# Moving a DMA transpose of two steps in four past the output projection, and packing the last output projections into a 64-column pass and a 32-column pass

## Chip, cores, metric

The kernel runs on one core of one Trainium2 chip. The metric is the device time of one execution in microseconds, the median over several runs. The core has five engines that are named here by their short names: PE (matrix multiply; "PEld" is its weight load), DVE (vector), ACT (activation), POOL (general purpose) and SP (sync). SP computes nothing; it issues DMAs in order. POOL's queue also issues DMAs in this kernel. Each engine works through its own list in order and waits on semaphores.

## What is computed

One sequence of 2048 tokens, width 640, goes through two blocks. The first is an attention with a recurrent memory of 8 tokens: the sequence is cut into 64 segments of 32 tokens, and each segment needs the memory that the segment before has produced.

```python
for s in range(n_seg):                       # 64 segments, one after the other
    h = concat([mem, xs])                    # 8 memory tokens + 32 tokens
    q, k, v = h @ Wq, h @ Wk, h @ Wv         # 640 -> 32 heads of 128
    p = softmax(mask(q @ k.T * Dh ** -0.5))
    o = (p @ v) @ Wo                         # 32*128 -> 640
    mem = o[:8]                              # goes into the next segment
    outs.append(o[8:])
h  = x + outs                                # x was layer-normed before attention
h2 = h + (relu(ln(h) @ W_gate) * (ln(h) @ W_up)) @ W_down   # 640 -> 1728 -> 640
```

All tensors are bf16. [...]W_gate, W_up and W_down are loaded over the attention weights at the end.

## The kernel before

**How the program is made.** Every instruction is recorded by `add(engine, function, reads, writes)`. `solve` turns the reads and writes into semaphore waits, and `run` gives each engine its instructions in the order in which they were recorded. So the order in the source is the order on each queue, and there is no scheduler. Most copies have line L461 (ACT) or L463 (DVE), most DMAs L357, and the DMA transposes L360, because helpers record them: tell them apart by their tiles.

**A step.** The loop `for s in range(NSEG)` (L893) does one segment per step; steps 2 to 62 take 13.1 to 14.9 us each. PE's order in a step is: K projection of the memory tokens and of 24 "rider" tokens of later segments (`project(a, ks, 1, ...)`), Q projection, two fifths of the V projection, `pick_mem` (takes the memory's queries out of `tok`), the rest of V, `scores`, a filler in five parts, `pv_mem`, `trans_om`, the output projection `wo_pass` (L641, 128 matmuls of 160 columns, four side by side in 32-column tiles), and `pv_x`. The filler differs by s % 4: for 2, 3 and 0 it is the K, Q and V projection of 32 extra tokens (`extra_units`), for 1 it is `woe_pass`, the output projection of the first 8 tokens of four earlier segments.

**Instruction lines.** PE's program is cut into lines of 256 instructions that are loaded while it runs (queue 8 of the trace, 16,384 bytes each). `align` pads the program so that a line ends at a chosen place in each `wo_pass`: after 98 of its 256 instructions for s % 4 = 1, after 111, 123 and 146 for 2, 3 and 0.

**The riders' queries.** A step projects the queries of its riders into two PSUM banks, `to_tok` copies them to `tok[2]` (ACT) and `tok[3]` (DVE), the DMA transpose `trans_q` turns these into `QS` (32 heads, 32 tokens), and `evac_q` copies the riders' part on ACT into the ring `Qr`, from which `scores` reads it two steps later or more. In SP's queue a step has three transposes in this order: `KS` (keys), `oT` (attention output of the step before, from `ox`), `QS`; then the loads of `loads()`. On ACT, `evac_q` stands after `exp_x` of the same step. `tok[2]` and `tok[3]` are written again by `extra_units` in steps with s % 4 = 2 and 3, and by the next step's Q projection in all steps. `QS` is used once more by the extra tokens' queries: transposed at the end of a step with s % 4 = 3 and copied in the next by the `late_q` list. The `late` list holds what is recorded just after the next step's `trans_ox`.

**The end of the attention.** Step 62 issues `load_gate_up` on POOL's queue: `xn2T`, `Wg`, `Wu`. Step 63 has K and V projections only. After its `pv_x` come: the output projection of segment 62 (`wo_pass` with `QS`, in two halves), the first gate and up product `gate_up(0, 0)`, the output projection of segment 63 (`wo_pass` with `oT`), `gate_up(0, 1)`, the first 8 tokens of segments 60 to 63 (`woe_pass` with `oTe`), `gate_up(0, 2)`, and then the gated block without a break, four blocks of 512 tokens. The stores to `attn_d` go through POOL's queue, and `ln2_load` fetches rows of it for the gated block.

Of the kernel before, what the change touches and what calls it, by code (L numbers as in the profile page):

```python
# [5 lines left out]
BF16 = mybir.dt.bfloat16  # L6
# [35 lines left out]
class _Graph:  # L42
# [164 lines left out]
def build_kernel(nc, A_x, A_mem0, A_Wq, A_Wk, A_Wv, A_Wo, A_seg_len, B_W_gate, B_W_up, B_W_down, out):  # L207
    _, S, D = A_x.shape
# [60 lines left out]
    act_e = [ar.alloc(f"act_e{i}", [128, DC, 32], BF16) for i in range(2)]  # L269
    tokp = [ar.alloc(f"tok{i}", [128, 1024], BF16) for i in range(2)]  # L270
    tok = [tokp[i // 2][:, 512 * (i % 2):512 * (i % 2) + 512] for i in range(4)]
# [25 lines left out]
    def bank(b):  # L297
        return ps[:, b * 512:(b + 1) * 512]
# [17 lines left out]
    def B(n):  # L316
        return ("B", n)
# [317 lines left out]
    def wo_pass(bk, mark=None, src=oT, keys=((("oT", "m"), ("oT", "x")), (("oT", "n"),)), halves=(0, 1)):  # L635
        for hf in halves:
            def f(pe, hf=hf):
                for hb in ORDER[16 * hf:16 * hf + 16]:
                    w = Wo[:, head_of(hb), :].rearrange("p (c g j) -> p g c j", g=4, j=32)
                    for gg in range(4):  # L640
                        i = pe.matmul(bank(bk)[32 * gg:32 * gg + 32, 0:160], src[:, hb, :], w[:, gg],  # L641
                                      start=(hb == ORDER[0]), stop=(hb == ORDER[31]), skip_group_check=True)
                return i
            op = add("pe", f, r=list(keys[hf]) + [("Wo", hf)], w=[B(bk)])
            if hf == 0:
                op.mark = mark

    def woe_pass(bk, part):

        def f(pe):  # L650
            for i in part:
                for q in range(4):
                    hb = 16 * (q // 2) + i
                    w = Wo[:, head_of(hb), :].rearrange("p (c g j) -> p g c j", g=4, j=32)
                    ins = pe.matmul(bank(bk)[32 * q:32 * q + 32, 0:320], oTe[:, hb, :],  # L655
                                    w[:, 2 * (q % 2):2 * (q % 2) + 2], start=(i == 0), stop=(i == 15),
                                    skip_group_check=True)
            return ins
        add("pe", f, r=oTe_keys + [("Wo", 0), ("Wo", 1)], w=[B(bk)])

# [41 lines left out]
    def trans_pe(dst, keys):  # L702

        flat = ox[:].rearrange("p k g d -> p (k g d)")
        for n, (b, eng) in enumerate(((T0, "act"), (T1, "dve"))):
            def f(pe, n=n, b=b):
                for k in range(4):
                    o = 512 * n + 128 * k
                    ins = pe.matmul(bank_bf(b)[:, k * 128:(k + 1) * 128], flat[:, o:o + 128], ident[:, :],
                                    is_transpose=True)  # L710
                return ins
            add("pe", f, r=[("ox", 0), ("ox", 1), ("ident",)], w=[B(b)])
            copy_op(eng, dst[:, 16 * n:16 * n + 16, :], slots(b, 0, 32)[:, 0:16, :], [B(b)], keys)

# [5 lines left out]
    def attn_keys(i):  # L720
        return [("attn", s) for s in range(4 * i, 4 * i + 4)] + [("attne", i, dg) for dg in range(2)]

# [162 lines left out]

    def woe_store(b):
        for dg in range(2):
            dma(bass.AP(attn_d, 128 * b * D + 320 * dg, [[SEG * D, 4], [D, M], [1, 320]]),
                bass.AP(at, 32 * dg * D, [[D, 32], [1, 320]]), r=[("at",)] + [("attn", 4 * b + j) for j in range(4)],
                w=[("attne", b, dg)], eng="pool")  # L890

    late, late_q = [], []
    for s in range(NSEG):  # L893
# [20 lines left out]
        if s > 0:  # L914
# [20 lines left out]
            late_q = []  # L935
            if nr and s < NSEG - 2:
                trans_q()
# [137 lines left out]

    def rows(bk, p, s):
        wo_rows(bk, wtok[p], ("wtok", p), "act")
        store_attn(wtok[p], ("wtok", p), s)

# [11 lines left out]
    mask_x()  # L1091
    trans_pe(QS, [("QS",)])
    pv_x(s, P0)
    copy_op("act", oTe[:, :, M * ((s - 1) % 4):M * ((s - 1) % 4) + M], QS[:, :, 0:M], [("QS",)], [("oTe", (s - 1) % 4)])
    norm_x(P0)
    wo_pass(BQ[1], None, QS, [[("QS",)]] * 2, (0,))
    trans_pe(oT, [("oT", "m"), ("oT", "n"), ("oT", "x")])
    wo_pass(BQ[1], None, QS, [[("QS",)]] * 2, (1,))
    rows(BQ[1], 0, s - 1)
    copy_oTe(s)  # L1100
    gate_up(0, 0)
    for i in range(4, 8):
        ln2_load(i)
    dma(h_rows[0][:, :, :], h_d[:, :].rearrange("(u p) d -> p u d", p=128), r=[("h_d", u) for u in range(4)] +
        [("Wdone", 1), ("Wu", DC - 1)], w=[("h", 0, u) for u in range(4)], eng="pool")
    dma(Wd[:, 0:FC - 1, :], B_W_down[0:FM, :].rearrange("(j p) d -> p j d", p=128),
        r=[("Wdone", 1)], w=[("Wd", 0)], eng="pool")
    dma(Wd[FR:128, FC - 1, :], B_W_down[FM:F, :], r=[("Wdone", 1)], w=[("Wd", 1)], eng="pool")
# [92 lines left out]
```

## Time and profile before

| | |
|---|---|
| runs | 1108.61, 1108.92, 1111.25 us; median 1108.92 |
| profiled execution | 1111.65 us, of it the span on the core 1109.9 us |
| mean granted PE clock | 0.992 |
| PE busy | 1054.9 us, 95% of the span |
| DVE, ACT, POOL busy | 608.7, 365.7, 290.5 us |
| DMA transposes and other DMAs of SP and ACT (queue 1) | 267,824 packets, 41.2% of the 16 DMA engines' time |
| steps with s % 4 = 1, 2, 3, 0 | median 13.98, 13.63, 13.34, 13.37 us from the end of one `pv_x` to the next |
| end of the last `pv_x` | 917.06 us; the gated block runs without a break from 932.94 us |

The page has one profiled execution. A group is a line with its engine, its output and inputs, its shape and count, the union of its busy time and the mean of one. "Idle before" is time in which the engine stood still before instructions of the group, with what ended it; "issue" means that nothing in the profile ended it. In the chain of waits, a row is the start, the length, and what took it. PE overlaps matmuls, so "PE busy" is not PE at its peak. Times "into the step" below count from the end of the `pv_x` before.

### The profile page before, as it was taken

To read this page: it belongs to the slowest core of one execution; us is meant where nothing else is said; L and a number is where in the kernel's file an instruction comes from. 1 tells how busy PE (TensorE), PEld (TensorE's weight loads), DVE (VectorE), ACT (ScalarE), POOL (GpSimd) and SP (SyncE) were. 2 spreads that over 40 slices of the span, in tenths; PEclk is the share of its full clock that TensorE was granted. 3 is DMA by queue.
4 is the path that set the end of the run, shared out by engine and by line. 5 is a ranking of instruction groups with operands and counts; after the bars stand their busy time and mean duration, and the time that the engine had idled before them with its cause. 6 is when DMAs were issued, how large, how long until landed. Compare 5 with 4: busy or idle time off the path is not lost.

```text
span 1109.9 us, 56106 instructions
## 1 busy us (share of the span) xinstructions
PE 1054.9 (95%) x28040; PEld 510.8 (46%) x23478; DVE 608.7 (55%) x1673; ACT 365.7 (33%) x794; POOL 290.5 (26%) x583
## 2 busy tenths in 40 slices
PE   4679999999999999999999999999999998999998
PEld 3344544444545454545454445444444454444443
DVE  3245656565556565666666666565656553553532
ACT  1214333433343433333334333334333332231211
POOL 1013333333333332323232323232324151000000
PEclk9979999999999999999999999999999999999999
DMA  9936464646463636465756665554545557132100
GB/s 362 377 84 111 88 109 89 105 90 107 81 110 80 115 79 110 83 123 100 119 103 116 104 114 107 93 92 97 94 92 96 93 159 240 39 80 75 27 18 25
DMA packets 287788, 121.65 MB, mean 110 GB/s; under 512 B 263968, under 2 KB 277184, under 8 KB 287552
## 3 DMA queue, kind: packets, MB, share of 16 engines
q1 hardware_dynamic: 267824, 93.92, 41.2%
q0 software_dynamic: 19312, 23.89, 9.3%
q8 instruction: 202, 3.31, 1.2%
q14 instruction: 34, 0.28, 0.1%
q10 hardware_dynamic: 416, 0.26, 0.1%
HBM read 36.79 MB, written 7.21 MB: 40 GB/s over the span
## 4 chain that ended last, share of the span: by engine, by line
PE 86%; DMA 8%; SPq 3%; issue 1%; POOL 1%; DVE 1%; ACT 1%; DVEq 0%; ACTq 0%
PE ps L419 24%; PE ps L397 23%; PE ps L641 13%; PE ps L1030 10%; PE ps L655 3%; PE ps L679 3%; PE ps L569 3%; PE ps L1062 3%; DMA Wo<-in_A_Wo_dram 3%; SPq L357 3%; PE ps L606 2%; DMA QS<-tok 2%; DMA KS<-tok 2%; PE ps L450 2%; PE ps L621 1%
## 5 line engine op out<-in xcount | busy, mean ns | idle before, releaser
L419 PE MATMUL ps<-W,act_r 128*32 128x512 bf16 x4277 | 399.1, 384 | 8.8 <-DMA W<-in_A_Wv_dram 2.5
L397 PE MATMUL ps<-W,act_r 128*32 128x512 bf16 x3603 | 356.9, 379 | 0.3
L357 POOL DMA_DIRECT2D Vr<-Vp x376 | 187.6, 506 | 449.7 <-ACT Px L588 396.9
L419 PEld LDWEIGHTS ps<-W,act_r 128*32 128x32 bf16 x4277 | 121.5, 97 | 262.2 <-issue 170.2
L461 ACT ACTIVATE tok<-ps 128x512 bf16<-128x512 f32 x191 | 110.3, 594 | 237.2 <-PE ps L397 204.7
L641 PE MATMUL ps<-Wo,oT 128*32 128x160 bf16 x8192 | 161.8, 236 | 14.6 <-DMA Wo<-in_A_Wo_dram 8.0
L641 PEld LDWEIGHTS ps<-Wo,oT 128*32 128x32 bf16 x8192 | 147.0, 98 | 36.6 <-issue 16.7
L463 DVE CAST tok<-ps 128x512 bf16<-128x512 f32 x131 | 90.5, 691 | 131.5 <-PE ps L397 109.9
L461 ACT ACTIVATE Qr<-QS 128x512 bf16<-128x512 bf16 (+3 forms) x107 | 70.1, 682 | 61.0 <-DMA QS<-tok 60.5
L419 PE MATMUL ps<-W,act_e 128*32 128x512 bf16 x900 | 89.6, 381 | 0.0
L397 PE MATMUL ps<-W,act_e 128*32 128x512 bf16 x900 | 89.1, 379 | 0.0
L552 DVE STREAM_TRANSPOSE TBf<-ps 128x64 f32<-128x64 f32 (+1 forms) x128 | 33.5, 262 | 93.9 <-PE ps L641 93.8
L694 DVE TENSOR_TENSOR ox<-ps,rx 128x512 bf16<-128x512 f32 x128 | 82.4, 685 | 2.2
L461 ACT ACTIVATE Vp<-ps 128x256 bf16<-128x256 f32 (+1 forms) x126 | 48.5, 385 | 104.7 <-PE ps L397 102.2
L357 POOL DMA_DIRECT2D attn_d<-wtok x64 | 46.6, 728 | 126.8 <-ACT wtok L461 126.6
L1045 DVE TENSOR_TENSOR hT<-g,ps 128x512 bf16<-128x512 bf16 (+1 forms) x56 | 38.5, 688 | 53.7 <-PE ps L1030 49.8
L1030 PE MATMUL ps<-xn2T,Wu 128*128 128x512 bf16 x260 | 64.6, 379 | 0.0
L1030 PE MATMUL ps<-xn2T,Wg 128*128 128x512 bf16 x246 | 61.6, 379 | 1.1 <-issue 0.3
L1043 ACT ACTIVATE g<-ps 128x512 bf16<-128x512 f32 (+1 forms) x56 | 32.4, 592 | 89.4 <-PE ps L1030 89.4
L397 PE MATMUL ps<-Wd,hT 128*128 128x320 bf16 x224 | 61.0, 299 | 0.0
L1062 PE MATMUL ps<-Wd,hT 128*128 128x320 bf16 x224 | 61.0, 299 | 0.0
L463 DVE CAST Vp<-ps 128x512 bf16<-128x512 f32 x64 | 44.2, 691 | 30.4 <-PE ps L397 24.5
(114 smaller groups left out, 1145.8 us busy)
## 6 DMA issues: line engine op xcount, KB each, us to landing
Vr<-Vp POOLq DMA_DIRECT2D x124, 48.8 KB, 2.3
W<-in_A_Wk_dram SPq DMA_DIRECT2D x2, 2560.0 KB, 13.2
W<-in_A_Wq_dram SPq DMA_DIRECT2D x2, 2560.0 KB, 29.3
W<-in_A_Wv_dram SPq DMA_DIRECT2D x2, 2560.0 KB, 28.1
Wo<-in_A_Wo_dram SPq DMA_DIRECT2D x2, 2560.0 KB, 28.5
xt<-in_A_x_dram SPq DMA_DIRECT2D x30, 160.0 KB, 3.6
Vr<-Vp POOLq DMA_DIRECT2D x128, 32.5 KB, 1.9
attn_d<-wtok POOLq DMA_DIRECT2D x64, 40.0 KB, 2.9
```

The costliest lines, as they stand in the source:

```text
L357: add(eng, lambda e: e.dma_start(dst, src), r=r, w=w, dma=True)
L397: return pe.add_instruction(mybir.InstMatmult(name=nc.get_next_instruction_name(), engine=mybir.EngineType.PE, ins=[pe.lower_ap(rhs), pe.l ...
L419: ins = pe.matmul(*a, start=(c == 0), stop=(c == DC - 1), skip_group_check=True)
L461: add("act", lambda a: a.activation(dst, src, ACTF.Copy), r=r, w=w)
L463: add("dve", lambda v: v.tensor_copy(dst, src), r=r, w=w)
L552: add("dve", lambda v, lo=lo, hi=hi: v.transpose(TBf[:, lo:hi, :].rearrange("p c t -> p (c t)"), src[:, 32 * lo:32 * hi]), r=[wkey], w=[(" ...
L569: i = pe.matmul(bank((P0, P1)[g % 2])[p:p + (M if a else 32), 40 * k:40 * k + 40], lh, Qr[:, h, q, :], start=True, stop=True, skip_group_c ...
L641: i = pe.matmul(bank(bk)[32 * gg:32 * gg + 32, 0:160], src[:, hb, :], w[:, gg], start=(hb == ORDER[0]), stop=(hb == ORDER[31]), skip_group ...
L694: add("dve", lambda v, kh=kh: v.tensor_tensor(ox[:, :, kh, :], src[:, :, kh, 0:128], ap(rx, kh, [[2, 4], [0, 128]]), ALU.mult), r=[B(b0 + ...
L1030: ins = pe.matmul(bank(bk), w[:, c, lo:lo + 128], xn2T[par][:, c, :], start=(c == 0), stop=(c == DC - 1))
L1045: add("dve", lambda v: v.tensor_tensor(hT[par][lo:128, j, :], g1[gi][lo:128, :], bank(bu)[lo:128, :], ALU.mult), r=[B(bu), ("g1", gi)], w= ...
L1062: i = pe.matmul(*a, start=(j == 0), stop=(j == FC - 1), skip_group_check=True)
```

## The change

Three things are changed in the loop (items 1 to 3), and the end of the attention is rewritten (item 4).

1. In steps with s % 4 = 0 and 1, `trans_q` is recorded after the store of `wo_pass`'s rows instead of after the Q projection, and it waits for the first copy of the new memory into `act_r` (key `"m"`). Its `evac_q` moves into a new list, `late_k`, which the next step records just after its K projection's two `to_tok` copies.
2. The store of `woe_pass`'s rows goes into `late`, so into the next step, and waits for that step's `KS`.
3. In step 62 `load_gate_up` is recorded after `wo_pass` and waits for its first half.
4. After the last `pv_x`, segment 62's 32 tokens and the first 8 tokens of segments 60 and 61 are put side by side into one 64-column tile, `wide`, which lies over the four `tok` buffers. Its product with Wo is 64 matmuls of 320 columns, two side by side. Segment 63 takes `woe_pass` with `oT`. The two `gate_up` products that stood between come after, and `ln2_load`, the load of `h` and of `Wd` wait for the sum `at` of segment 63.

```diff
-    tokp = [ar.alloc(f"tok{i}", [128, 1024], BF16) for i in range(2)]
+    tokb = ar.alloc("tok", [128, 2048], BF16)
+    tokp = [tokb[:, 1024 * i:1024 * i + 1024] for i in range(2)]
...
-    def trans_q():
+    def trans_q(after=()):
         dma_t(QS[:].rearrange("p h t -> p (h t)").rearrange("p (k r) -> p k r", r=128), tokp[1][:, :],
-              [("tok", 2), ("tok", 3)], [("QS",)])
+              [("tok", 2), ("tok", 3)] + list(after), [("QS",)])
...
     def ln2_load(i):
         u = i % 4
-        dma(xt2[u][:, :], x_ap[128 * i:128 * i + 128, :], r=[("Wdone", 1), ("Wu", DC - 1)], w=[("xt2", u)])
+        dma(xt2[u][:, :], x_ap[128 * i:128 * i + 128, :], r=[("Wdone", 1), ("at",)], w=[("xt2", u)])
...
             to_tok(BQ[0], 0, "act")
             to_tok(BQ[1], 1, "dve")
+            for f in late_k:
+                f()
+            late_k = []
...
-            if nr and s < NSEG - 2:
+            qlate = nr and s % 4 < 2
+            if nr and not qlate and s < NSEG - 2:
                 trans_q()
...
-                if s < NSEG - 2:
+                if s < NSEG - 2 and not qlate:
                     evac_q(QS, ("QS",), t0, nr, M, "act")
...
-        if s == NSEG - 2:
-            load_gate_up([("oTe", (s - 1) % 4)])
...
-            woe_store(s // 4 - 1)
+            late.append(lambda b=s // 4 - 1: woe_store(b, [("KS",)]))
         wo_pass(T1, MARKS[s % 4] if s > 0 else None)
+        if s == NSEG - 2:
+            load_gate_up([("oTe", (s - 1) % 4), ("go", T1, 0)])
         to_act(s + 1, B(T1), bank(T1)[:, 0:160])
         if s >= 1:
             wo_rows(T1, wtok[s % 2], ("wtok", s % 2), "act")
             store_attn(wtok[s % 2], ("wtok", s % 2), s - 1)
+            if qlate and s < NSEG - 2:
+                trans_q([("act", (s + 1) // 4 % 2, (s + 1) % 4, "m")])
+                late_k.append(lambda t0=t0, nr=nr: evac_q(QS, ("QS",), t0, nr, M, "act"))
         pv_x(s, P0)
...
+    def wo_wide(bk, part):
+            for hb in part:
+                w = Wo[:, head_of(hb), :].rearrange("p (c g j) -> p g c j", g=4, j=32)
+                for i in range(2):
+                    ins = pe.matmul(bank(bk)[64 * i:64 * i + 64, 0:320], wide[:, hb, :], w[:, 2 * i:2 * i + 2],
+                                    start=(hb == 0), stop=(hb == H - 1), skip_group_check=True)
...
     mask_x()
-    trans_pe(QS, [("QS",)])
+    copy_op("dve", wide[:, :, SEG:SEG + 2 * M], oTe[:, :, 0:2 * M], oTe_keys, [("wide", 1)] + toks)
+    trans_pe(wide[:, :, 0:SEG], [[("wide", 0)], [("wide", 2)]])
     pv_x(s, P0)
-    copy_op("act", oTe[:, :, M * ((s - 1) % 4):M * ((s - 1) % 4) + M], QS[:, :, 0:M], [("QS",)], [("oTe", (s - 1) % 4)])
     norm_x(P0)
-    wo_pass(BQ[1], None, QS, [[("QS",)]] * 2, (0,))
-    trans_pe(oT, [("oT", "m"), ("oT", "n"), ("oT", "x")])
-    wo_pass(BQ[1], None, QS, [[("QS",)]] * 2, (1,))
-    rows(BQ[1], 0, s - 1)
-    copy_oTe(s)
+    wo_wide(BQ[1], range(16))
+    trans_pe(oT, [[("oT", "m"), ("oT", "x")], [("oT", "n")]])
+    wo_wide(BQ[1], range(16, 32))
+    copy_op("act", xt[:, 0:320], bank(BQ[1])[:, 0:320], [B(BQ[1])], [("xt",)])
+    store_seg(s - 1, lambda dg: bass.AP(xt, 64 * dg * D, [[D, 32], [1, 320]]), ("xt",))
+    for dg in range(2):
+        dma(bass.AP(attn_d, SEG * (s - 3) * D + 320 * dg, [[SEG * D, 2], [D, M], [1, 320]]),
+            bass.AP(xt, (64 * dg + 32) * D, [[D, 16], [1, 320]]), r=[("xt",)] + [("attn", s - 3 + j) for j in range(2)],
+            w=[("attne", NSEG // 4 - 1, dg)], eng="pool")
+    woe_pass(P3, range(16), oT, [("oT", "m"), ("oT", "n"), ("oT", "x")])
+    woe_sum(P3)
+    store_seg(s, lambda dg: bass.AP(at, 32 * dg * D, [[D, 32], [1, 320]]), ("at",))
     gate_up(0, 0)
+    gate_up(0, 1)
     for i in range(4, 8):
         ln2_load(i)
...
-    wo_pass(P0)
-    rows(P0, 1, s)
-    gate_up(0, 1)
-    woe_pass(P3, range(16))
-    woe_sum(P3)
-    woe_store(NSEG // 4 - 1)
     gate_up(0, 2)
```

More of the change, by code (lines that the diff above doesn't have):

```diff
@@ L643, in f, with woe_pass @@
                 return i
-            op = add("pe", f, r=list(keys[hf]) + [("Wo", hf)], w=[B(bk)])
+            op = add("pe", f, r=list(keys[hf]) + [("Wo", hf)], w=[B(bk), ("go", bk, hf)])
             if hf == 0:
                 op.mark = mark
-    def woe_pass(bk, part):
+    def woe_pass(bk, part, src=oTe, keys=oTe_keys):
         def f(pe):
@@ L654, in f @@
                     w = Wo[:, head_of(hb), :].rearrange("p (c g j) -> p g c j", g=4, j=32)
-                    ins = pe.matmul(bank(bk)[32 * q:32 * q + 32, 0:320], oTe[:, hb, :],
+                    ins = pe.matmul(bank(bk)[32 * q:32 * q + 32, 0:320], src[:, hb, :],
                                     w[:, 2 * (q % 2):2 * (q % 2) + 2], start=(i == 0), stop=(i == 15),
@@ L658, in f @@
             return ins
-        add("pe", f, r=oTe_keys + [("Wo", 0), ("Wo", 1)], w=[B(bk)])
+        add("pe", f, r=list(keys) + [("Wo", 0), ("Wo", 1)], w=[B(bk)])
     def wo_rows(bk, dst, dkey, eng):
@@ L712, in trans_pe @@
             add("pe", f, r=[("ox", 0), ("ox", 1), ("ident",)], w=[B(b)])
-            copy_op(eng, dst[:, 16 * n:16 * n + 16, :], slots(b, 0, 32)[:, 0:16, :], [B(b)], keys)
+            copy_op(eng, dst[:, 16 * n:16 * n + 16, :], slots(b, 0, 32)[:, 0:16, :], [B(b)], keys[n])
     def copy_oTe(s):
@@ L720, in attn_keys @@
     def attn_keys(i):
-        return [("attn", s) for s in range(4 * i, 4 * i + 4)] + [("attne", i, dg) for dg in range(2)]
+        return [("attn", s) for s in range(4 * i, 4 * i + 4)] + [("attne", i, dg) for dg in range(2)] + (
+            [("attn", t, 1) for t in (NSEG - 2, NSEG - 1)] if 4 * i + 4 == NSEG else [])
     def add_attn(h, x, a, r, w):
@@ L732, in ln2_load @@
         u = i % 4
-        dma(xt2[u][:, :], x_ap[128 * i:128 * i + 128, :], r=[("Wdone", 1), ("Wu", DC - 1)], w=[("xt2", u)])
-        load_attn(at2[u], i, [("Wdone", 1), ("Wu", DC - 1)], ("at2", u))
+        dma(xt2[u][:, :], x_ap[128 * i:128 * i + 128, :], r=[("Wdone", 1), ("at",)], w=[("xt2", u)])
+        load_attn(at2[u], i, [("Wdone", 1), ("at",)], ("at2", u))
     def ln2_front(i):
@@ L884, in woe_sum, with woe_store @@
             r=[B(bk), ("at",)], w=[("at",)])
-    def woe_store(b):
+    def woe_store(b, after=()):
         for dg in range(2):
             dma(bass.AP(attn_d, 128 * b * D + 320 * dg, [[SEG * D, 4], [D, M], [1, 320]]),
-                bass.AP(at, 32 * dg * D, [[D, 32], [1, 320]]), r=[("at",)] + [("attn", 4 * b + j) for j in range(4)],
+                bass.AP(at, 32 * dg * D, [[D, 32], [1, 320]]), r=[("at",)] + [("attn", 4 * b + j) for j in range(4)] + list(after),
                 w=[("attne", b, dg)], eng="pool")
-    late, late_q = [], []
+    late, late_q, late_k = [], [], []
     for s in range(NSEG):
@@ L1074, in build_kernel, with f, store_seg @@
     s = NSEG - 1
-    def rows(bk, p, s):
-        wo_rows(bk, wtok[p], ("wtok", p), "act")
-        store_attn(wtok[p], ("wtok", p), s)
+    wide = tokb[:].rearrange("p (h t) -> p h t", t=2 * SEG)
+    toks = [("tok", t) for t in range(4)]
+    def wo_wide(bk, part):
+        def f(pe):
+            for hb in part:
[3 more added lines that the diff above has]
+                                    start=(hb == 0), stop=(hb == H - 1), skip_group_check=True)
+            return ins
+        add("pe", f, r=[("wide", 0), ("wide", 1), ("wide", 2), ("Wo", 0), ("Wo", 1)], w=[B(bk)])
+    def store_seg(t, rows, skey):
+        for dg in range(2):
+            dma(bass.AP(attn_d, SEG * t * D + 320 * dg, [[D, SEG], [1, 320]]), rows(dg), r=[skey],
+                w=[("attn", t, 1) if dg else ("attn", t)], eng="pool")
     a, ks, kn = pass_act(s)
@@ L1091, in build_kernel @@
     mask_x()
-    trans_pe(QS, [("QS",)])
+    copy_op("dve", wide[:, :, SEG:SEG + 2 * M], oTe[:, :, 0:2 * M], oTe_keys, [("wide", 1)] + toks)
+    trans_pe(wide[:, :, 0:SEG], [[("wide", 0)], [("wide", 2)]])
     pv_x(s, P0)
-    copy_op("act", oTe[:, :, M * ((s - 1) % 4):M * ((s - 1) % 4) + M], QS[:, :, 0:M], [("QS",)], [("oTe", (s - 1) % 4)])
     norm_x(P0)
-    wo_pass(BQ[1], None, QS, [[("QS",)]] * 2, (0,))
-    trans_pe(oT, [("oT", "m"), ("oT", "n"), ("oT", "x")])
-    wo_pass(BQ[1], None, QS, [[("QS",)]] * 2, (1,))
-    rows(BQ[1], 0, s - 1)
-    copy_oTe(s)
+    wo_wide(BQ[1], range(16))
[3 more added lines that the diff above has]
+    store_seg(s - 1, lambda dg: bass.AP(xt, 64 * dg * D, [[D, 32], [1, 320]]), ("xt",))
+    for dg in range(2):
+        dma(bass.AP(attn_d, SEG * (s - 3) * D + 320 * dg, [[SEG * D, 2], [D, M], [1, 320]]),
[4 more added lines that the diff above has]
+    store_seg(s, lambda dg: bass.AP(at, 32 * dg * D, [[D, 32], [1, 320]]), ("at",))
     gate_up(0, 0)
+    gate_up(0, 1)
     for i in range(4, 8):
@@ L1104, in build_kernel @@
     dma(h_rows[0][:, :, :], h_d[:, :].rearrange("(u p) d -> p u d", p=128), r=[("h_d", u) for u in range(4)] +
-        [("Wdone", 1), ("Wu", DC - 1)], w=[("h", 0, u) for u in range(4)], eng="pool")
+        [("Wdone", 1), ("at",)], w=[("h", 0, u) for u in range(4)], eng="pool")
     dma(Wd[:, 0:FC - 1, :], B_W_down[0:FM, :].rearrange("(j p) d -> p j d", p=128),
-        r=[("Wdone", 1)], w=[("Wd", 0)], eng="pool")
-    dma(Wd[FR:128, FC - 1, :], B_W_down[FM:F, :], r=[("Wdone", 1)], w=[("Wd", 1)], eng="pool")
-    wo_pass(P0)
-    rows(P0, 1, s)
-    gate_up(0, 1)
-    woe_pass(P3, range(16))
-    woe_sum(P3)
-    woe_store(NSEG // 4 - 1)
+        r=[("Wdone", 1), ("at",)], w=[("Wd", 0)], eng="pool")
+    dma(Wd[FR:128, FC - 1, :], B_W_down[FM:F, :], r=[("Wdone", 1), ("at",)], w=[("Wd", 1)], eng="pool")
     gate_up(0, 2)
```

## Prediction

> **What bounds the kernel.** I read the page's busy times, PE's waits, the chain of waits in single steps, and then SP's and ACT's timelines.
>
> ```profile
> span 1109.9 us, 56106 instructions
> ...
> PE 1054.9 (95%) x28040; PEld 510.8 (46%) x23478; DVE 608.7 (55%) x1673; ACT 365.7 (33%) x794; POOL 290.5 (26%) x583
> ...
> PEclk9979999999999999999999999999999999999999
> ...
> PE 86%; DMA 8%; SPq 3%; issue 1%; POOL 1%; DVE 1%; ACT 1%; DVEq 0%; ACTq 0%
> ```
>
> PE bounds it, at full clock, and 86% of the chain is PE's own work. The change removes almost no PE work, so what it can win is PE's idle time. Of PE's own waits (us in total, times, longest):
>
> ```profile
> PE ps L641 <- issue: 8.1, 15, 2.4
> ...
> PE ps L569 <- DMA KS<-tok: 1.9, 3, 1.1
> ```
>
> The first row is `wo_pass` standing still for nothing that the profile names. In step 41 (s % 4 = 1) the chain of waits puts it 48 matmuls into the pass (start, us, what):
>
> ```profile
> 618.13 0.96 PE ps L641 x48
> 619.09 0.55 issue
> 619.65 1.49 PE ps L641 x74
> ```
>
> `align` ends an instruction line 98 instructions, or 49 matmuls, into this pass: PE waits for its next line. Queue 8's packets in the trace say why it is late. The line's packet starts 9.72 us into step 41 and ends at 10.64; the pass goes on at 12.08, 1.4 us later. In step 17 it starts at 8.75, and the pass takes 2.39 us without a gap. Before it, SP's timeline has
>
> ```profile
> 614.07 1.26 SPq L360 DMA_TRANSPOSE QS<-tok  x1
> ```
>
> issued 6.5 us into the step and landed at 9.57; its packets fill the 16 DMA engines from 1.0 us after the issue to 3.1 us after it. In most steps the line's packet starts just when they end: the fetch stands behind `QS`.
>
> Other steps show what a late transpose does to the next step. In step 15 `Kr<-tok` still reads `tok` when ACT wants to write it:
>
> ```profile
> 259.67 0.60 ACT L461 ACTIVATE tok<-ps 128x512 bf16<-128x512 f32 x1 [2.37 <-DMA Kr<-tok]
> ```
>
> `pick_mem` waits for this copy, and PE stood still for 0.74 us. How long `QS` takes, over the whole run:
>
> ```profile
> DMA to landing us min/median/max: 3.0/3.2/5.5
> ```
>
> At the end of the attention PE's timeline shows:
>
> ```profile
> 919.25 0.94 PE L641 MATMUL ps<-Wo,QS 128*32 128x160 bf16 x43
> 922.55 0.58 PE L641 MATMUL ps<-Wo,QS 128*32 128x160 bf16 x21 [2.37 <-issue]
> 923.29 1.03 PE L1030 MATMUL ps<-xn2T,Wg 128*128 128x512 bf16 x4 [0.16 <-DMA Wu<-in_B_W_up_dram]
> ...
> 930.42 2.36 PE L655 MATMUL ps<-Wo,oTe 128*32 128x320 bf16 x64
> 932.94 0.38 PE L1030 MATMUL ps<-xn2T,Wg 128*128 128x512 bf16 x1 [0.16 <-issue]
> ```
>
> The longest gap of the kernel is again a line that comes late: its packet starts only at 920.08, while the load of `Wg` and `Wu` fills the DMA engines.
>
> **The change part by part.**
>
> *`QS` out of the way of the line (steps s % 4 = 0, 1).* A clean `wo_pass` is 2.39 us. What the passes of the 15 later steps of each kind take beyond that, summed from the trace, is 6.7 us for s % 4 = 1 (ten of them 0.25 to 1.0 each) and 1.7 for 0 (four of 0.37 to 0.46). Without `QS` the line's packet should start 0.7 us earlier: step 62, which has no `QS`, starts it 0.5 us after its scores begin, steps with `QS` after about 1.5, and 0.3 of that difference is its shorter program. A start at 9.0 us or before left no gap, and all late starts but one were at 10.0 or before, so nearly all gaps go; I take 85% of 8.4: -7.1. What is late next is PE itself. Step 37 began 0.82 us late because ACT's copies of the extra values stood behind an `evac_q` that waited for `QS` (landed at 11.96 in step 36); it moves away: -0.8.
>
> Here a rule speaks against all of this. The trace first: 15 waits, 8.1 us, always at a line's end. The Trainium skill, "Runtime: NRT & Kernel Launch", section "Instruction fetch mechanics", says that the sequencer refills 256-instruction blocks by its own DMA queue, and that crossing a block costs little and is mostly hidden. By the rule the moved transpose wins nothing, and the sum is the end's -3.7 and the costs below; by the trace it is -7.9 more. I take the trace, since the gap grows with the start of the packet. For s % 4 = 2 and 3 nothing is moved.
>
> *`QS` in its new place.* SP now waits for the first copy of the memory, which ends 0.05 us before the step ends (by DVE's timeline), so `QS` is issued at the next step's start, fills the DMA engines from about 1.0 to 3.1 us into it and lands at 3.0 to 3.3 in the good case. Behind it on SP is `KS`, which waits for K's copies and is issued at 3.1 as before. In steps with s % 4 = 3, where `at<-xt` is already in flight at that time, `KS` landed 6.1 to 7.3 us into the step against 6.1 to 6.6 in steps with 0 and 1, and scores begin at 6.9: 0 in most steps. In steps 32, 36, 40 and 44 a transpose `at<-xt` stands behind the waiting `QS`; its reader is SP's store in the next step, after 6 us, so no cost. The loads in steps with s % 4 = 0 and 1 are issued 1.3 us earlier, no cost. The line fetched at the step's start ends its packet at 0.0 to 0.7 us, before `QS` moves bytes: no cost.
>
> Two queues wait for the landing. `evac_q` stands on ACT before the copy into `tok[2]`, and both copies into `tok` now wait until `QS` has been read out. ACT's `tok` copy starts 4.5 us into a clean step and may start at 4.6 without delay to `pick_mem`. `evac_q` takes 0.84 us in the step after s % 4 = 0 (one piece) and 0.94 after s % 4 = 1 (two); there also the two small `row_rstd` activations (0.5 us) follow it. So the latest landing that costs nothing is about 3.7 and 3.4 us. The good case fits by 0.1 to 0.6 us. But of the 62 landings that the trace tells, 24 took 3.8 us or more and 18 took 4.5 or more, mostly where a line's packet got in between. A landing at 4.6 to 5.5 costs PE about 1.1 us. In the new place a line's packet starts at 2.8 to 3.6 us in steps with s % 4 = 1, when the transpose is nearly done, but at 2.4 to 3.1 in many steps with 2. Bounds: nothing, if none is slow (below nothing is excluded: nobody gets `QS` sooner than he needs it); 31 x 29% x 1.1 = 10 us, if it is slow as often as before. I take one in eight, 31 x 1/8 x 1.1 = +4.
>
> *`woe_store` into the next step.* 15 x 2 small DMAs. POOL waits for `KS` at 6.3 us; behind it are the rider's value DMAs, issued at 8.8 to 9.4, so 2 x 0.6 us fit. Zero; their packets leave the end of the step, which may help the line that steps with s % 4 = 2 wait for 1.1 to 1.9 us in (0.1 to 0.7 us each); between -3 and +1, taken as 0.
>
> *`load_gate_up` behind half a `wo_pass`.* POOL issued the first of it at 906.72; half the pass ends at 907.3, with the semaphore some 907.5. The load ends 0.8 us later, at about 924.0 in place of 923.2. Cover: the projections below.
>
> *The end.* From 917.06 on. A half of `wo_wide` is 32 matmuls of 320 columns, two side by side, so 16 rounds; by the nearest row, 64 such matmuls in 16 rounds of four took 2.36 us (L655), so 2.36: 919.4. The transposes of `ox` 0.62 (ready at 918.7): 920.0. Second half: 922.4. `woe_pass` with `oT`: 924.8. The line's end that cost 2.37 us falls now 43 matmuls into this pass, at 924.0, because fewer instructions stand ahead of it; its packet may come 0.8 us later than before, ready at 923.4: no wait. Weights have landed at 924.0. `gate_up(0, 0)` and `(0, 1)`, 2.16 us each as before, end at 929.2, where before 932.94 stood: -3.7. Bounds: if the line is 1 us later still, -3.0; if rounds of two are as short as a 320-column round can be by the pass of 160 columns (2 x 70 ns), -4.1. DVE's added copy into `wide` (0.3 us) ends before `pv_x` does. `ln2_load` and `Wd` start 2 to 3 us later; `Wd` is wanted at 953, and landed 14 us after its issue at 926.2 before, so at some 944 now: no cost. If the cover were gone, `down` would wait by as much as it is late.
>
> Sum: -7.1 - 0.8 + 4 - 3.7 = -7.6 us against the profiled execution's own 1111.65 us, span 1109.9. That execution is 2.7 us over the median; I take the difference over to the median: 1108.92 - 7.6 = 1101.3.
>
> **Rivals.**
>
> *Slow landings as often as before (17%).* The loop then wins 7.9 and pays 10, the end -3.7: 1107. For: the bimodal landings. Against: the line's packet comes at the transpose's end in half of the steps.
>
> *`QS` becomes the bound (10%): slower.* One mechanism: `QS` and the line's packet meet in nearly every step, `QS` lands near 5 us, `evac_q` and both `tok` copies wait, and PE stands still before `pick_mem`. For: in steps with s % 4 = 3, `at<-xt`, issued at 0.1 to 0.9 us, mostly landed at 5.2 to 6.3. Against: it starts behind `Kr`, `QS` starts behind nothing. At 1.1 us in 24 of 31 steps: +26 - 7.9 - 3.7, 1123. It decides above some 11 slow steps in 31, where 12 us of gain are eaten.
>
> *The line stays late (13%), as after the rule:* other DMAs (values, loads of x) delay it, and only the end wins; with +1 for landings 1106.
>
> **How the numbers follow.** The forecast itself has 60%, and reaches from 1095 (no slow landings, half a us more at the end) to 1105. A measurement of this kernel can tell about 0.3%, 3.3 us, from no change: below 1105.6 is faster, above 1112.2 slower. Faster: nearly all of the forecast (0.58), a quarter of the first rival, half of the last, 0.7 in all; slower: the second rival and a little of the first, 0.13; the rest, 0.17, is the same. Leaving out the second rival and the forecast's best end, the range is 1094 to 1109.
>
> **What would show it.** Right: `wo_pass` near 2.4 us in steps with s % 4 = 0 and 1, PE's row L641 <- issue below 2 us; `QS` landed by 3.4 us; ACT's `tok` copies waiting for PE, not for a DMA; no gap over 0.5 us between the last `pv_x` and `gate_up(0, 2)`, 12.2 us apart. Wrong: rows of ACT `tok` or `Qr` waiting for `QS` by more than 15 us with PE's L450 waiting for `tok`; or L641 <- issue still at 5 us.

## The result, and the profile after

| | before | after |
|---|---|---|
| median (range, runs) | 1108.82 us (1108.61 to 1111.25, 4) | 1101.38 us (1099.87 to 1103.7, 4) |
| ratio, 95% interval | | 0.993 (0.9904 to 0.9955) |
| profiled execution, span | 1111.65, 1109.9 us | 1099.96, 1098.2 us |

The change is 7.4 us faster; 7.6 were forecast. The changed kernel, measured again later beside other runs of the kernel before, gave 0.9943 (0.9925 to 0.9962, 15 runs). The two profiled spans are 11.7 us apart, because the profiled execution of before lay 2.7 us over its median and that of after 1.4 under.

In the changed kernel the line numbers are one to ten higher: `wo_pass` is L642, `woe_pass` L656, `pick_mem` L451, `scores` L570, the copies L462 (ACT) and L464 (DVE), the DMA transposes L361, gate and up L1039, `wo_wide` L1094. "Step" times count again from the end of the `pv_x` before. From the page of after, the span, the busy times and the chain by engine:

```profile
span 1098.2 us, 55733 instructions
...
PE 1048.2 (95%) x27862; PEld 505.5 (46%) x23286; DVE 608.5 (55%) x1673; ACT 365.6 (33%) x792; POOL 291.0 (26%) x585
...
PE 89%; DMA 6%; SPq 3%; DVE 1%; ACT 1%; issue 1%; DVEq 0%; ACTq 0%
```

PE still bounds the kernel. Of what it stood still for (us in total, times, longest), these rows of after matter:

```profile
PE ps L451 <- ACT tok L462: 3.5, 3, 1.5
PE ps L570 <- DMA KS<-tok: 3.4, 6, 0.7
...
PE ps L656 <- issue: 1.4, 1, 1.4
...
PE ps L642 <- issue: 0.4, 2, 0.3
```

The last row is `wo_pass` waiting for its line: 8.1 us in 15 waits before, 0.4 in two now. The first two rows are what was paid for it: `pick_mem` behind ACT's copy into `tok[2]`, which stands behind the moved `evac_q` (before had no such row); and `scores` behind a later `KS` (1.9 us before).

Split of the 11.7 us, from the ends of the `pv_x` groups: up to the last `pv_x` -8.1 (steps with s % 4 = 0, 1, 2 and 3: -3.8, -3.6, +0.1 and -0.4; step 1 -0.8; the rest +0.4), from there to `gate_up(0, 2)` -4.2, the rest of the gated block +0.6. The kind s % 4 = 0 also profits from chance: two waits of step 48, 1.4 us together, stood in the profiled execution of before and not in that of after.

The end, in PE's timeline of after (start, us, what):

```profile
908.88 2.36 PE L1094 MATMUL ps<-Wo,tok 128*64 128x320 bf16 x32
911.17 0.62 PE L710 MATMUL ps<-ident,ox 128*128 128x128 bf16 x8
911.72 2.36 PE L1094 MATMUL ps<-Wo,tok 128*64 128x320 bf16 x32
914.02 2.36 PE L656 MATMUL ps<-Wo,oT 128*32 128x320 bf16 x64
916.31 1.25 PE L1039 MATMUL ps<-xn2T,Wg 128*128 128x512 bf16 x5
...
920.63 0.81 PE L1039 MATMUL ps<-xn2T,Wg 128*128 128x512 bf16 x3
```

No row has an idle time behind it: the 2.37 us gap and the small ones are gone. The last `pv_x` ends at 908.95, and `gate_up(0, 2)` starts 11.68 us later; 12.2 were forecast, 15.88 it was.

How the moved `QS` lands, from the view of the tile `QS` in after (all its transposes), and one step in ACT's timeline in which it landed late:

```profile
  DMA QS<-tok: 23.3, 29
...
DMA to landing us min/median/max: 3.0/3.1/5.6
```

```profile
242.51 0.60 ACT L462 ACTIVATE tok<-ps 128x512 bf16<-128x512 f32 x1 [1.92 <-PE ps L398]
245.00 0.94 ACT L462 ACTIVATE Qr<-QS 128x256 bf16<-128x256 bf16 x2 [1.90 <-DMA QS<-tok]
245.85 0.28 ACT L376 ACTIVATE lv<-mv,eps 128x1 f32<-128x1 f32 x1
246.16 0.20 ACT L378 ACTIVATE rs<-lv 128x1 f32<-128x1 f32 x1
246.26 0.58 ACT L462 ACTIVATE tok<-ps 128x512 bf16<-128x512 f32 x1
```

ACT's waits for `QS` fell from 60.5 to 23.3 us. The second fence is step 14, which starts at 240.14. `QS` landed 4.84 into it, `evac_q` (the row `Qr`) and two small activations follow, and the `tok` copy that `pick_mem` needs starts at 6.12 where a clean step has 4.5. PE stood still for 1.50 us.

Of the six waits for `KS`, three (2.1 of the 3.4 us) lie in steps 33, 37 and 45 and come from SP's queue. In SP's timeline of after, step 37 (start 549.38):

```profile
549.34 1.24 SPq L361 DMA_TRANSPOSE QS<-tok  x1
550.62 1.28 SPq L361 DMA_TRANSPOSE at<-xt  x1
552.47 1.27 SPq L361 DMA_TRANSPOSE KS<-tok  x1
```

`at<-xt`, recorded in step 36, stood behind the waiting `QS` and was issued 1.24 us into step 37. `KS` was issued at 3.09 as ever, but `at<-xt` was still under way: it landed at 6.75, `KS` at 7.6, and `scores` waited for 0.67 us. In step 41 `at<-xt` had landed at 4.86; there `KS` landed at 6.29, and nothing waited.

### The profile page after: what moved, and what is told of

The parts are those of the page before. It is cut to its first block, busy times and chain, and to the rows that moved or that the text cites. A ratio compares the mean times of both kernels' runs of the same rounds, so it can differ in the third digit from the quotient of the medians.

```text
span 1098.2 us, 55733 instructions
## 1 busy us (share of the span) xinstructions
PE 1048.2 (95%) x27862; PEld 505.5 (46%) x23286; DVE 608.5 (55%) x1673; ACT 365.6 (33%) x792; POOL 291.0 (26%) x585
## 4 chain that ended last, share of the span: by engine, by line
PE 89%; DMA 6%; SPq 3%; DVE 1%; ACT 1%; issue 1%; DVEq 0%; ACTq 0%
PE ps L420 24%; PE ps L398 23%; PE ps L642 13%; PE ps L1039 11%; PE ps L656 3%; PE ps L680 3%; PE ps L570 3%; PE ps L1071 3%; DMA Wo<-in_A_Wo_dram 3%; SPq L358 3%; DMA KS<-tok 2%; PE ps L607 2%; PE ps L451 2%; DMA QS<-tok 1%; PE ps L622 1%
## 5 line engine op out<-in xcount | busy, mean ns | idle before, releaser
L420 PE MATMUL ps<-W,act_r 128*32 128x512 bf16 x4277 | 396.9, 382 | 6.5 <-DMA W<-in_A_Wv_dram 3.0
L420 PEld LDWEIGHTS ps<-W,act_r 128*32 128x32 bf16 x4277 | 119.3, 97 | 260.9 <-issue 166.0
L462 ACT ACTIVATE tok<-ps 128x512 bf16<-128x512 f32 x192 | 111.0, 594 | 217.4 <-PE ps L398 190.1
L642 PE MATMUL ps<-Wo,oT 128*32 128x160 bf16 x8064 | 155.7, 235 | 10.0 <-DMA Wo<-in_A_Wo_dram 8.8
L464 DVE CAST tok<-ps 128x512 bf16<-128x512 f32 x131 | 90.5, 691 | 126.4 <-PE ps L398 108.6
L642 PEld LDWEIGHTS ps<-Wo,oT 128*32 128x32 bf16 x8064 | 143.8, 98 | 29.0 <-DVE oT L464 16.2
L420 PE MATMUL ps<-W,act_e 128*32 128x512 bf16 x900 | 89.4, 381 | 0.0
L462 ACT ACTIVATE Vp<-ps 128x256 bf16<-128x256 f32 (+1 forms) x126 | 48.5, 385 | 104.8 <-PE ps L398 102.2
L462 ACT ACTIVATE Qr<-QS 128x512 bf16<-128x512 bf16 (+3 forms) x107 | 70.0, 682 | 25.8 <-DMA QS<-tok 23.3
L1039 PE MATMUL ps<-xn2T,Wg 128*128 128x512 bf16 x260 | 64.6, 379 | 0.0
L1039 PE MATMUL ps<-xn2T,Wu 128*128 128x512 bf16 x260 | 64.6, 379 | 0.0
L462 ACT ACTIVATE wtok<-ps 128x160 bf16<-128x160 f32 x62 | 18.8, 303 | 123.0 <-DVE TBf L553 123.0
```

The source lines that it names most:

```text
L420: ins = pe.matmul(*a, start=(c == 0), stop=(c == DC - 1), skip_group_check=True)
L462: add("act", lambda a: a.activation(dst, src, ACTF.Copy), r=r, w=w)
L464: add("dve", lambda v: v.tensor_copy(dst, src), r=r, w=w)
L1039: ins = pe.matmul(bank(bk), w[:, c, lo:lo + 128], xn2T[par][:, c, :], start=(c == 0), stop=(c == DC - 1))
```

## The experiments

The experiments were timed in four groups, each on another chip and with the kernel before beside it; ratios are to that kernel in the same group. Its medians were 1108.7 us (the first four experiments), 1108.3 (the change again and the three after it), 1107.2 (the three checks on the earlier slot) and 1107.9 (the last one).

### The two halves of the change

The end alone: the changed kernel with items 1 and 2 taken back.

```diff
-            qlate = nr and s % 4 < 2
+            qlate = False
...
-            late.append(lambda b=s // 4 - 1: woe_store(b, [("KS",)]))
+            woe_store(s // 4 - 1)
```

> The end of the attention as changed (wide pass, weights' load after half a wo_pass), the loop as before. By the prediction's sum: 3.7 us faster than before, 12.2 us between the last pv_x and gate_up(0, 2) where before took 15.9, and the loop's passes with their gaps as before (some 8 us beyond 2.39 in steps with s % 4 = 0 and 1). If the end only moves the wait for the line or for the weights, it is within 1 us of before.

The loop alone: the kernel before with items 1 and 2 put in.

> QS and the store of woe_pass's rows moved as in the change, the end as before. By the theory that QS holds back PE's instruction line: 3.5 to 7.5 us faster than before, wo_pass at 2.4 us in steps with s % 4 = 0 and 1. By the rule that line crossings are hidden anyway: not faster. The two halves e1 and e2 should add up to the change's 7.4 us.

| | median (range, runs) | ratio (95%) |
|---|---|---|
| end alone | 1103.64 (1098.38 to 1106.56, 11) | 0.9953 (0.9926 to 0.9979) |
| loop alone | 1106.58 (1104.53 to 1112.09, 14) | 0.9989 (0.9971 to 1.0006) |

The end is worth 5.1 us, the loop 2.2; they add up to 7.3, and the change measured 7.4. The loop's part alone can't be told from nothing. In `wo_pass` it did about half of what it was to do. PE's waits for a line there, in the profile of the end alone and of the loop alone (where `wo_pass` is L641):

```profile
PE ps L642 <- issue: 4.3, 9, 0.9
```

```profile
PE ps L641 <- issue: 5.7, 8, 2.7
```

Of the second row 2.7 us are the gap at the end of the attention, which that kernel keeps, so its loop has 3.0 where the kernel with the end alone has 4.3; the `wo_pass` of the kinds 0 and 1 took 3.4 us beyond a clean pass in the loop alone and 6.7 in the end alone. So a gain is there, and something eats a part of it.

### What the new place costs

The changed kernel, with the moved transposes left out from step 4 on. `evac_q` copies stale data then, and nothing waits for a transpose.

```diff
-                trans_q([("act", (s + 1) // 4 % 2, (s + 1) % 4, "m")])
+                if s < 4:
+                    trans_q([("act", (s + 1) // 4 % 2, (s + 1) % 4, "m")])
```

> The changed kernel with the moved QS transposes left out from step 4 on (evac_q copies what an earlier transpose left in QS, so those riders' queries are stale). If the new place is not free, this shows its price: by the theory some 4 to 6 us faster than the changed kernel, with no wait of PE for ACT's tok copies and none of scores for KS in steps 33, 37 and 45. If QS costs nothing where it is now, the time is the changed kernel's within 1 us.

1095.62 us (1093.59 to 1097.79, 4 runs), ratio 0.9886 (0.9855 to 0.9917). Against the end alone, of the same group, that is 8.0 us: what the transposes cost in their old place (here they are not moved but gone, with their packets). Against the changed kernel, measured in two other groups (ratios 0.993 and 0.9943), it is 5 to 6 us: an estimate of what they cost in their new place, uncertain by 3 to 4 us, for this kernel has four runs. Its waits of PE:

```profile
PE ps L642 <- issue: 2.0, 5, 0.5
PE ps L570 <- DMA KS<-tok: 1.2, 3, 0.6
PE ps L451 <- ACT tok L462: 1.1, 1, 1.1
```

The third row is step 2, which still has its transpose. `pick_mem` behind ACT's `tok` fell from 3.5 to 1.1 us and `scores` behind `KS` from 3.4 to 1.2. These 4.6 us of waits are most of the estimate. The two profiled executions themselves are only 2.2 us apart, in part because `wo_pass` waited longer for lines in this one (2.0 us against 0.4).

### `at<-xt` ahead of `QS`

In steps 32, 36, 40 and 44 `at<-xt` is recorded before the waiting `QS`.

```diff
             if qlate and s < NSEG - 2:
+                if n:
+                    dma_t(chunks_of(at[:, :])[:, :, 0:n], xt[0:n, :], [("xt",)], [("at",)])
                 trans_q([("act", (s + 1) // 4 % 2, (s + 1) % 4, "m")])
...
         if n:
-            dma_t(chunks_of(at[:, :])[:, :, 0:n], xt[0:n, :], [("xt",)], [("at",)])
+            if not (s and qlate):
+                dma_t(chunks_of(at[:, :])[:, :, 0:n], xt[0:n, :], [("xt",)], [("at",)])
```

> The changed kernel, but in steps 32, 36, 40 and 44 the transpose at<-xt stands ahead of QS in SP's queue, not behind it. The changed kernel's scores wait 0.7 us for KS in steps 33, 37 and 45. If that is because at<-xt now runs after QS just before KS, these waits go, and the time is 2.5 to 3.5 us less than the changed kernel's. If KS is late there for another cause (the store to xn2_d, the load of x), nothing changes.

1108.3 us (1103.31 to 1115.19, 22 runs), ratio 0.9998 (0.9981 to 1.0016): the whole gain is gone, where 2.5 to 3.5 us more were expected. SP's timeline of step 37 (start 550.07), and PE's waits:

```profile
548.39 2.06 SPq L361 DMA_TRANSPOSE at<-xt  x1
550.50 1.30 SPq L361 DMA_TRANSPOSE QS<-tok  x1
553.16 2.35 SPq L361 DMA_TRANSPOSE KS<-tok  x1
```

```profile
PE ps L451 <- ACT tok L462: 11.7, 7, 2.2
PE ps L570 <- DMA KS<-tok: 0.8, 2, 0.6
```

The part about `KS` was right: its row falls from 3.4 to 0.8. What I had not reckoned with is that SP was busy with the issue of `at<-xt` for 2.06 us. `QS` was issued 0.43 into the step in place of -0.04 (0.26 to 0.72 in the four steps) and landed at 5.26 to 6.06, in place of 3.0 to 3.1, in all four. `pick_mem` waited for 1.4 to 2.2 us in each of steps 33, 37, 41 and 45, 7.3 us in all; three more late landings, in steps that the edit does not touch (2, 46 and 50), cost 4.4. Two of these steps, 2 and 46, were late in the change too, for 2.1.

### A later `evac_q`

The next group had the changed kernel again, that kernel with `late_k` run after the Q projection's `to_tok` copies and not after those of the K projection, and a kernel that has this and leaves `QS` in its old place in steps 32, 36, 40 and 44 (by the edit that the last experiment shows).

```diff
-            for f in late_k:
-                f()
-            late_k = []
...
-            for f in late_q:
+            for f in late_k + late_q:
                 f()
-            late_q = []
+            late_k, late_q = [], []
```

> The changed kernel itself, on the chip of the next three and beside runs of the kernel before: 6 to 9 us faster than before, as measured first (7.4).

> The changed kernel, but the next step records evac_q after its two copies into tok[2] and tok[3], not before them. These copies then wait for the landing of QS alone, not also for 0.84 to 0.94 us of evac_q. By the theory that slow landings (3 of 29 in the changed kernel's profile) cost PE landing plus evac_q: PE's waits for ACT's tok copies (3.5 us) fall below 2 us, and the time by 1 to 2 us. If the copies are held by something else, no change.

> As e6, and in steps 32, 36, 40 and 44 QS stays where it was before the change, so that at<-xt is issued at 11.6 us into the step and not behind QS. By the theory that the moved at<-xt makes KS late in steps 33, 37, 41 and 45 (0.8 us each): no wait of scores for KS there, 2 to 3 us less than e6, so some 3 to 5 us less than the changed kernel. The last trial (at<-xt ahead of a moved QS) took KS's waits away too, but made QS land 2 us late; here QS is not moved in these four steps, so it should not.

| | median (range, runs) | ratio (95%) |
|---|---|---|
| the change again | 1100.71 (1095.23 to 1107.95, 15) | 0.9943 (0.9925 to 0.9962) |
| `evac_q` later | 1107.0 (1100.62 to 1111.26, 22) | 0.9982 (0.9968 to 0.9995) |
| `evac_q` later, four steps at the old place | 1106.51 (1099.22 to 1112.6, 22) | 0.9986 (0.9972 to 1.0001) |

Both are about 6 us slower than the change, where a gain was expected. PE's waits in the change again:

```profile
PE ps L451 <- ACT tok L462: 4.1, 4, 1.6
PE ps L570 <- DMA KS<-tok: 3.1, 8, 0.6
...
PE ps L642 <- issue: 1.8, 4, 0.6
```

and in the kernel with the later `evac_q`:

```profile
PE ps L570 <- DMA KS<-tok: 3.2, 7, 0.8
...
PE ps L642 <- issue: 2.9, 9, 0.5
...
PE ps L420 <- issue: 2.2, 3, 1.3
```

The row of `pick_mem` behind ACT's `tok` is no longer in the list, as expected. In its place there are more waits for lines: 2.9 us in `wo_pass`, now mostly in steps with s % 4 = 1 and 2, and 2.2 in the projections (L420), 1.9 of them in step 55. (This profiled execution took 1103.26 us, 3.7 under that kernel's median, so its rows hold only part of the loss.)

### An earlier slot

The changed kernel, but `QS` waits only for the end of `mask_x`, 11.3 us into its own step.

```diff
-                trans_q([("act", (s + 1) // 4 % 2, (s + 1) % 4, "m")])
+                trans_q([("Px",)])
```

> The changed kernel, but the moved QS waits for the end of mask_x (11.3 us into the step) and not for the memory's copy (13.2), so it goes 2 us earlier and moves its bytes from 12.3 to 14.4, when PE's next line is fetched (12.1 to 13.9). By the theory that line and QS get in each other's way: lines ready later, PE standing still 1.1 to 2 us into the steps with s % 4 = 2 and 1, 6 to 20 us slower than the changed kernel. By the rule that line crossings are hidden: not slower, or a little faster, since QS lands well before it is wanted.

1096.41 us (1094.46 to 1098.63, 5 runs), ratio 0.9896 (0.9878 to 0.9915). My own expectation was a loss of several us; it was clearly wrong. SP's timeline around the start of step 37 (545.64):

```profile
543.60 1.24 SPq L361 DMA_TRANSPOSE QS<-tok  x1
544.88 1.84 SPq L361 DMA_TRANSPOSE at<-xt  x1
548.73 1.58 SPq L361 DMA_TRANSPOSE KS<-tok  x1
```

`QS` is issued 2.04 us before the step ends. Over all its transposes `QS` takes longer than in the change (3.7 us in the median in the repeat below, 3.1 there), since a line's packet is on its way at the same time (in all of the 56 known landings of a moved `QS` in the two profiles of this slot, and in 12 of 58 in the two of the change), but it lands 1.5 to 3.3 us into the next step, before its readers want it. No wait of `pick_mem` for ACT's `tok` is left, and none for `KS` in steps 33, 37, 41 and 45. So the meeting costs the reader of `QS` nothing where it has slack. The line does pay at times: `woe_pass` stood still for one in step 57, for 1.25 us.

### Three checks on the earlier slot

On a third chip: the earlier slot with `woe_store` back at its old place, the earlier slot with the later `evac_q`, and the earlier slot again.

> The kernel with QS's transpose issued at the end of mask_x (11.3 us into the step), and woe_store back at its old place, the end of the step s % 4 = 1. If the store's packets hold back the line that the following step s % 4 = 2 waits for at the end of wo_pass, that step's wo_pass gaps come back (2 to 4 us in all) and QS, in flight at the same time, lands later: 2 to 4 us above the early-slot kernel's 1096.4. If moving the store is worth nothing, as the prediction took it, the time stays within 1.5 us of 1096.4.

> The kernel with QS's transpose issued at the end of mask_x, and evac_q of the moved QS behind ACT's and DVE's second pair of tok copies, as in the run with evac_q later. In the early-slot kernel QS has landed before the first tok copies, so evac_q's place no longer decides about pick_mem. If the 6 us lost by the later evac_q came from what it pushes back in its own step (the step's own QS transpose, which may not overwrite QS before evac_q has read it, is issued 0.2 us later in steps s % 4 = 2 and then meets the line for wo_pass), the loss comes back here: 1100 to 1103, with wo_pass gaps in steps s % 4 = 2 of 3 us or more. If it came from QS in flight across the step's boundary, it is gone: 1096 to 1098.

> The early-slot kernel once more, on the same chip as the two others, as their measure. If its gain over the change was not one chip's: 1095 to 1098, ratio to the kernel before 0.988 to 0.992. If it was chance of that call, 1100 to 1102 as the change itself.

| | median (range, runs) | ratio (95%) |
|---|---|---|
| earlier slot, `woe_store` at its old place | 1100.87 (1095.23 to 1102.44, 9) | 0.9941 (0.9913 to 0.9968) |
| earlier slot, `evac_q` later | 1110.82 (1103.69 to 1117.52, 22) | 1.003 (1.0011 to 1.0049) |
| earlier slot again | 1101.48 (1096.66 to 1107.85, 21) | 0.9951 (0.9935 to 0.9968) |

The repeat does not confirm the gain: 0.9951 now, 0.9896 before, with intervals that do not touch, for the same kernel. The first had five runs and another chip. The two profiled executions differ mostly in PE's waits for lines (its rows that end in "issue"), 3.2 us in the first and 9.7 in the repeat. The change gave 0.993 and 0.9943; it ran on the same chip as the slot only the first time, and there the slot was 4.3 us faster. The earlier slot is as good as the change; whether it is better is open.

`woe_store` makes no difference that these runs can tell (0.9941 and 0.9951).

The later `evac_q` costs 9 us here, so its loss did not come from the crossing of the step's boundary. One cause lies in the same step. In step 30 (s % 4 = 2), ACT's and then SP's timeline of the changed kernel, where the step starts at 455.03:

```profile
458.15 0.93 ACT L462 ACTIVATE Qr<-QS 128x256 bf16<-128x256 bf16 x2 [0.16 <-DMA QS<-tok]
...
464.01 0.94 ACT L462 ACTIVATE Qr<-QS 128x512 bf16<-128x512 bf16 x2 [0.17 <-DMA QS<-tok]
```

```profile
460.83 1.25 SPq L361 DMA_TRANSPOSE QS<-tok  x1
```

and the same rows of the earlier slot with the later `evac_q`, where it starts at 457.36:

```profile
462.43 0.93 ACT L462 ACTIVATE Qr<-QS 128x256 bf16<-128x256 bf16 x2
...
468.54 0.94 ACT L462 ACTIVATE Qr<-QS 128x512 bf16<-128x512 bf16 x2 [2.31 <-DMA QS<-tok]
```

```profile
463.43 1.23 SPq L361 DMA_TRANSPOSE QS<-tok  x1
```

The first row of each is the moved `evac_q`. It ends 4.05 us into the step in the one and 6.00 in the other. The step has a second transpose into `QS`, its own, which may not overwrite `QS` before that: it is issued at 5.80 in the one and 6.07 in the other. PE's `scores` begin at 6.88 and 6.91, and the packet of the next line follows them (in these steps of the changed kernel 1.5 us later in the median): the lead of `QS` over them shrinks from 1.08 to 0.84 us. The second `evac_q` can start 8.98 us into the step in the one and 11.18 in the other. Over all steps with s % 4 = 2 whose landing the trace tells, the step's own `QS` took over 4.5 us from issue to landing in 13 of 28 in the three kernels with a later `evac_q`, and in 1 of 50 in the changed kernel (two profiles) and the other three with the earlier slot. By the lead it is cleaner still. Over all 14 profiles, 1 of the 102 landings was that slow where `QS` was issued more than 0.9 us before the step's scores, and 16 of 32 where it was less. With it the line for `wo_pass` starts its packet later: 9.06 to 9.21 in the median of the three, 8.46 to 8.91 in the five.

The shorter lead is not `evac_q`'s doing alone: in step 30 SP itself was free only at 5.94, since the issue of `KS` took 1.48 us in place of 1.23. In nine of the 13 slow landings `evac_q` ended after SP was free, in four before. And the account holds for s % 4 = 2 only, where `wo_pass` took 3.0 us over a clean pass in all, against 0.7 in the repeated earlier slot. More was lost in steps with s % 4 = 1, where the step's own `QS` is issued only at 11.3 us: 3.7 against 1.7 us in `wo_pass`, and 5.5 against 3.5 of waiting for a line in `woe_pass`. The cause of that part is open.

### `QS` at its old place in four steps only

The changed kernel, with `qlate` false in steps 32, 36, 40 and 44.

```diff
-            qlate = nr and s % 4 < 2
+            qlate = nr and s % 4 < 2 and e2b is None
```

> The change, but in steps 32, 36, 40 and 44, where at<-xt stands behind QS on SP, QS keeps its old place and its evac_q too; evac_q of the other moved steps stays ahead of the tok copies. By my theory KS is no longer held up in steps 33, 37, 41 and 45 (scores wait 0.7 each less), and wo_pass of the four steps pays 0.4 at most as before: 1 to 3 us less than the change, ratio to the kernel before 0.990 to 0.994, and no wait of scores for KS in those steps. By the rival, that the loss of the combined run came from QS's old place in these four steps and not from the later evac_q, it is slower than the change: 0.997 to 1.000.

1103.77 us (1099.57 to 1106.15, 14 runs), ratio 0.9962 (0.9942 to 0.9982): between the two forecasts, and its interval overlaps the change's. PE's waits:

```profile
PE ps L451 <- ACT tok L462: 6.3, 5, 2.1
...
PE ps L570 <- DMA KS<-tok: 1.2, 4, 0.5
```

The row of `KS` fell from 3.4 to 1.2 us, with none left in steps 33, 37, 41 and 45. But in this execution five of the 25 landings of a moved `QS` that the trace tells were late, and cost 6.3 us. Whether the edit is worth 2 us can't be told from under that scatter.

## Why the prediction came out

**`QS` out of the way of the line: -7.1 forecast.** Right. `wo_pass` of the kinds 0 and 1 took 8.3 us over a clean pass before and 1.5 and 1.7 in the two profiles of the change: -6.8 and -6.6. The line's packet starts 1.5 and 1.6 us after the scores begin in the two kinds, where it was 2.2 before (medians), so 0.6 earlier; 0.7 was forecast. In times, clearing the old place was worth 8.0 us (end alone against transposes left out), where -7.1 - 0.8 = -7.9 stood; that these two agree so well is luck, for in the profiles of those two kernels `wo_pass` accounts for 3.2 us only (6.7 and 3.5 over a clean pass), and as much was won between the scores and `pv_mem`. Step 37 begins without a gap, as forecast. The rule of the Trainium skill, "Runtime: NRT & Kernel Launch", section "Instruction fetch mechanics", that crossing a block of instructions is mostly hidden, would have given nothing here; the row of waits and the times speak for the trace.

Two readings were too simple. The chain's row of 48 matmuls in step 41 starts 0.17 us after the pass; by PE's timeline the gap comes after 54 of the 128 (in step 5 after 49), so the line's end drifts somewhat over the run. And the packets of `QS` end some 2.6 us after its issue (median of 24 landings without other loads), not 3.1. In step 41, the example, those up to 9.7 us are the store `xn_d<-at`, which SP issues behind `QS`, and the line's packet starts when they end. In 18 of the 30 steps with s % 4 = 0 and 1 it starts within 0.3 us of the end of `QS`; in step 49 it came 1.7 us after it, with the DMA engines idle. So `QS` was the main cause of late lines, not the only one.

**Late landings: +4 forecast, "one in eight" at 1.1 us.** Right in number and price, but one in eight was a guess between two bounds, and that it came out is luck. Late were 3 of 29 known landings in the first profile of the change, 4 of 29 in its second and 5 of 25 in the kernel with four steps at the old place: 12 of 83, one in seven. They cost 13.9 us by the rows of `pick_mem`, 1.2 each. Nor are they spread evenly: 11 of the 12 fall in steps with s % 4 = 2, and steps 2 and 46 are late in all three profiles. The latest landing without cost was put at 3.4 us in steps with s % 4 = 2: a landing at 4.84 cost 1.50 and one at 3.9 cost 0.56, so it is 3.34. The rival with `QS` as the bound did not happen, but its mechanism is real: the run with `at<-xt` ahead brought it about in four steps with a shift of 0.3 to 0.8 us.

**`KS` and `at<-xt`: "no cost" forecast.** This step failed. I had regarded the reader of `at`, and not what `at<-xt`, issued 1.24 us into the next step, does to the transfer behind it. It holds up `KS`: 0.71, 0.67 and 0.67 us in steps 33, 37 and 45, and in none of them where `at<-xt` goes ahead of `QS`, where `QS` keeps its old place, or in the earlier slot. Step 41 lost 1.37 to a line in `woe_pass` instead; that this has the same cause is not shown. The new place cost an estimated 5 to 6 us in place of the 4 in the sum.

**The end: -3.7 forecast.** Right in kind, a little too small: -4.2 in the profiles, just beyond its own bound of -4.1, and -5.1 in the medians of the end alone, with an interval (-2.3 to -8.2) that takes in the forecast. The path from the last `pv_x` is 11.68 us in place of 12.1, mostly because each group of matmuls starts some 0.06 before the one ahead of it ends, and the sum laid them end to end. The line at matmul 43 of `woe_pass` brought no wait, as worked out.

**`woe_store`: 0, and `load_gate_up` 0.8 later: no cost.** The first agrees with the run that put it back in the earlier slot. For the second nothing waited at `gate_up(0, 0)`.

So the total, -7.6 against -7.4, is closer than its parts are known. By the medians the loop won 2.2 us (-0.7 to 3.2) in place of 3.9, and the end 5.1 in place of 3.7: two errors that cancel, if they are errors. By the two profiles the loop won 8.1, but these executions lie some 4 us further apart than the medians. To agree within 0.2 us is luck.

## What to carry to other kernels

When a transfer is moved within a step, ask two things of every queue that it joins: what now stands behind it, and whether its buffer's next writer must wait longer. Here the transfer behind it (`KS`), the issue ahead of it (`at<-xt`) and the next writer (the step's own `QS`) cost some 2, 7 and 6 us, where the loop as a whole won 2.2.

A transfer that meets other traffic need not cost anything if its reader has slack: the earlier slot met a line every time and was no slower than the change, which met one in a fifth of the cases. And a difference of half a per cent between two versions needs both on the same chip and more than a handful of runs: the same kernel gave 0.9896 on one chip with five runs and 0.9951 on another with 21.

## What was not expected of the hardware

- A shift of a quarter of a us in an issue goes with another landing: in steps with s % 4 = 2, `QS` issued 1.08 us before the scores took some 3.2 us, and issued 0.84 before them it took over 4.5 in half of the steps. The trace tells where the time goes. It has 16 signals for a landing. In all 17 of these slow landings (14 profiles) at least 12 of the 16 came within 3.6 us; the last packets of the transpose started within 0.07 us of the end of a line's packet, which had taken 0.9 to 1.4 us, and the last signal came 1.0 to 1.1 us after them. In none of the 477 landings of `QS` under 3.4 us did its last packet start so close behind a line's. So a small part of the transpose waits behind the line, and all of it is late. Why the last signal takes 1.1 us there and mostly 0.5 elsewhere is not shown.
- SP's issue of a transpose takes 1.24 us or up to 2.7: `at<-xt` took 1.28 in the change and 2.06 in the kernel where it comes first. What SP issues next is late by that.
- In some steps with s % 4 = 1 a line's packet that mostly starts at 2.9 to 3.7 us started at 6.6 to 7.0, and `woe_pass` stood still for 0.7 to 1.4 us: step 41 of the change, step 25 of the later `evac_q`, and ten steps of the four kernels with the earlier slot, five of them with the later `evac_q`. In these ten the line before it had started at 0.05 to 0.5 us, where -1.2 to 0 is usual; in the other two at -0.58. No run tested the cause.
